# Batch two's first block by fp32 products and TensorE transposes, loads ahead queued behind the bias tiles, the DMA queue in source order later, z shared evenly

## The chip, the cores and the metric

One core of a Trainium2 chip runs the whole program. The metric is the device time of one execution in microseconds, and the median of several runs is quoted. TensorE (PE, with its weight loads as PEld), VectorE (DVE), ScalarE (ACT) and GpSimd (POOL) each run their own instruction stream; SyncE (SP) issues nearly all transfers. Sixteen DMA engines serve the core.

## The reference

The program is attention with a learned bias over relative position, followed by a two-layer network. There are 4 batches, 8 heads, 576 tokens and 64 channels per head.

```
scores = q @ k.T / 8 + bias[head]          # bias = relu(x @ w1 + b1) @ w2, x = log1p|i-j| / log1p(max(i,1))
attn   = exp(scores - max) / (sum + 1e-9)
x      = (attn @ v), heads side by side    # 2304 tokens x 512
h      = x @ w_in                          # 512 -> 2048
out    = (h * clip(h + 3, 0, 6) / 6) @ w_out   # 2048 -> 512
```

All inputs and the output are fp32; the two weight matrices arrive as float64 and are turned into pairs of fp16 parts inside the program.

## The kernel before, in words

**Tiles.** Heads go in four pairs `p`. Attention is cut into units `(b, p, u)`: block `u=0` holds the first 256 tokens of a batch, `u=1` the other 320. All `u=0` units of the four batches come first, then all `u=1` units. A `u=0` unit has four softmax tiles of 128 rows by 576 keys, a `u=1` unit has five, so tiles are numbered n = 0 to 143: batch one's first block is n = 0 to 15, batch two's first block n = 16 to 31, all first blocks end at n = 63.

**A tile on the split path** (all but n = 0 to 15): q and k are split into two fp32r parts (`split_qk_a` on ACT, `split_qk_b` on POOL), the scores are three products (`qk_step`), `soft_max` on DVE adds the bias and finds the row maximum, `soft_exp` on ACT takes the exponent, `soft_norm` and `soft_low` write the normalised tile as two fp16 parts (`hl`: one part by ACT or POOL, the other by DVE, after two small DVE steps), `soft_turn` transposes them by DMA into `at`, and `pv_step` multiplies by v, which is split too (`split_v_a`, `split_v_b`, with two DMA copies). `x_high` and `x_low` write x as two fp16 parts.

**A tile on the direct path** (`direct(b, p, t)`, n = 0 to 15): fp32 products of q and k as loaded (`load_qk0`), the same softmax steps, then five TensorE transposes of the unnormalised tile into PSUM and one ACT copy to SBUF (`soft_low`), and fp32 products with v (`pv_first`). The row sums are inverted for four tiles at once and spread by four small products; `x_first` multiplies.

**Bias.** The bias rows are made in 36 groups of 16 query rows: four `z` tiles (a relu of 128 by 576, by ACT or DVE as the strings `z0`, `z1`, `zeng` say: `z_group`), sixteen TensorE passes (`bias_mm`), an ACT evacuation and a store to DRAM (`bias_out`). Groups 0 to 15 are made before the first tile, beside the preparation of `w_in`. The other 20 are needed only from n = 64 on. They are made by `steps(gen_b, ...)`, 1.1 half steps a tile, two half steps a group, once `phase` is 2; what is missing when the first `u=1` bias tile is to be loaded, at n = 59, is made there at once (`bias_until(S)`). `load_bias` fetches bias tiles up to six tiles ahead.

**The network.** `ffn(b, u)` is a generator: 16 steps of 12 products into `h_ps` and 16 steps of 12 products into `o_ps`, with ACT, DVE and POOL steps (`post`) between them. The block of (0, 0) starts at n = 21 with 4 steps a tile; at its step "w2" the rest of `w_out_prep` is drained. Later blocks go at 2 steps a tile, and 1.55 from n = 64 on. What is not done after the last tile is run at the end.

**Order.** A list scheduler with modelled durations orders each engine's instructions by program order and readiness; it may pull a later instruction forward when the model says that its inputs are there. From n = 21 on TensorE alone keeps program order (`in_order`). At the same point PSUM changes from three double banks for attention and two single banks for the network (`open_psum(stack_p, 3, 2)`) to two and four.

Of the kernel before, what the change touches and what calls it, by code (L numbers as in the profile page):

```python
# [18 lines left out]
S = 576  # L19
# [7 lines left out]
VC = 5 * 128  # L27
CFG = {'z0': 'AD', 'gz': 4, 'z1': 'AAAD', 'gz2': 16, 'zeng': 'AD', 'sg': 'P', 'wm1': 'A', 'wm2': 'A', 'hl': 'AP', 'gl': 'PP', 'vm': 'A', 'g0': 16, 'rwi': 3.0, 'rw0': 1.0, 'rw1': 1.3, 'ro': 3.0, 'rb': 1.1, 'rf0': 4.0, 'rf': 2.0, 'rf1': 1.55, 'la': 6, 'gq': 2, 'gap': -8.0, 'wu': 8, 'act': '', 'tv': 'A', 'pw': 0, 'po': 0, 'gr': 'AD'}
F64_BIAS = 2.0 ** -112
# [4 lines left out]
def attention_moe_kernel(  # L34
# [47 lines left out]

    out_open = [False, 0]
    queue = []
# [12 lines left out]
    eye_sb = const.tile([128, 128], F32, name="eye_sb")  # L97
    r_sb = const.tile([128, 2, PAIRS * 4], F32, name="r_sb")
    wi = big.tile([128, 2, KC, DFF], F16, name="wi")
# [63 lines left out]
    def v_scale(b):  # L163
        parts = const.tile([128, PAIRS], F32, tag="vparts", name="vparts")
        for p in range(PAIRS):
            t = st_p.tile([128, VC], F32, tag="vs", bufs=2, name="va")
            dq("v").dma_start(out=t, in_=vp[b, p])
# [187 lines left out]

    def load_qk0(p):
        t = qk_p.tile([128, 512 + S], F32, tag="hi", name="qk0")
        q, k = t[:, 0:512].rearrange("p (a b) -> p a b", a=2), t[:, 512:512 + S]
        for s in range(2):
            rows = slice(64 * s, 64 * s + 64)  # L360
            dq("q").dma_start(out=q[rows, s], in_=qk[0, p][rows, 0:256])
            nc.gpsimd.memset(q[rows, 1 - s], 0.0)
        dq("q").dma_start(out=k, in_=qk[0, p][:, 256:256 + S])
        qk_t[0, p, 0] = (t, k)

# [41 lines left out]
    def load_v(b, p, u):  # L407
        if (b, u) == (0, 0):
# [3 lines left out]
        dq("v").dma_start(out=t, in_=vp[b, p])  # L412
        v_t[b, p, u] = t
# [24 lines left out]
    def load_bias(b, p, i):  # L438
# [19 lines left out]
        if i < 4:  # L458
            for r in range(2):
                rows = slice(64 * r, 64 * r + 64)  # L460
                if (p, i) not in KEEP:
                    dq("b").dma_start(out=out[rows], in_=bias_d[2 * i + r][:, 2 * p:2 * p + 2, :])
                    continue
                for s in range(2):
                    dq("b").dma_start(out=src[s][rows], in_=bias_d[2 * i + r][:, 2 * p + s, :])
        else:
            for s in range(2):
                dq("b").dma_start(
                    out=out[64 * s:64 * s + 64, 0:S], in_=bias_d[8][:, 2 * p + s, :]
                )  # L470
        return out, src

# [18 lines left out]
    def qk_step(n):  # L491
# [3 lines left out]
        if direct(b, p, t):  # L495
            ps = s_bank("s_ps")
            q, k = qk_t[0, p, 0]
            c = 256 * s + 128 * i
# [41 lines left out]
    def soft_exp(n):  # L540
        bt, sm = a_t[n]
        b, p, t = tiles[n]
        total = r_sb[:, 0, 4 * p + t:4 * p + t + 1] if direct(b, p, t) else sm[:, 1:2]
        nc.scalar.activation(  # L544
# [27 lines left out]
    def direct(b, p, t):  # L572
        return b == 0 and t < 4

# [51 lines left out]

    def pv_first(p):
        at, v = at_t.pop((0, p, 0)), v_t.pop((0, p, 0))
        n = 256
        ps = s_bank("pv_ps")  # L630
        for c in range(5):
            k = slice(64 if c == 4 else 0, 128)
            for s in range(2):
# [5 lines left out]
                )  # L639
        total, r = (r_sb[:, k, 4 * p:4 * p + 4] for k in range(2))  # L640
        nc.vector.tensor_scalar(out=total, in0=total, scalar1=1e-9, scalar2=None, op0=ALU.add)
        nc.vector.reciprocal(out=r, in_=total)
        for t in UT[0]:
# [4 lines left out]
            )  # L648
        pv_t[0, p, 0] = ps

    def x_first(p):
        ps = pv_t.pop((0, p, 0))
        n = 256
        x = x_tile(0, 0)
        xr = hl_p.tile([128, 2, n], F32, tag="hl", name="xr")
        xs, rb = xr[:, 0], xr[:, 1]
        nc.scalar.activation(
            out=rb, in_=ps[:, 1, 0:n], func=AF.Copy, scale=pscale["v0"][1]
        )
# [5 lines left out]
    def pv_step(b, p, u):  # L665
        if direct(b, p, 4 * u):
            return pv_first(p)
        at = at_t.pop((b, p, u))
# [14 lines left out]
    def x_high(b, p, u):  # L683
        if direct(b, p, 4 * u):
            return x_first(p)
        ps = pv_t[b, p, u]
# [203 lines left out]
    def front(n):  # L890
# [3 lines left out]
        if at(n):  # L894
            soft_max(n)
        if n == SWITCH:
            open_steady()
# [140 lines left out]
    phase = 0  # L1038
    SWITCH = 21
    in_order = tc.manual_schedule(engines={mybir.EngineType.PE})  # L1040

    def open_steady():
        nonlocal phase
        drain(gen_w)
        hidden_scale(0)
        for c in range(KC):
            xv = x_t[0, 0][:, :, c]
            nc.vector.tensor_scalar(
                out=xv, in0=xv, scalar1=pscale["r1"][:, c:c + 1], scalar2=None, op0=ALU.mult
            )  # L1050
        stack_a.close()
        del pools["a"], pools["w"]
        stack_p.close()
        open_psum(ctx, 2, 4)
# [4 lines left out]
        in_order.__enter__()  # L1059

    for g in range(cfg["g0"]):
# [3 lines left out]
        if 0 <= g - cfg["gq"] < PAIRS:  # L1065
            load_qk0(g - cfg["gq"])
# [31 lines left out]
    for q_ in queue:  # L1098
        drain(q_)
    in_order.__exit__(None, None, None)  # L1100

# [55 lines left out]
```

## Time and profile before

| what | value |
|---|---|
| median of 3 runs | 739.45 us (733.67 to 739.86) |
| profiled execution, its own time | 735.63 us |
| span of the profiled execution | 733.8 us, so 1.8 us lie around it |
| mean granted TensorE clock | 0.944 |
| PE busy | 639.8 us (87%), 5490 instructions |
| DVE busy | 504.9 us (69%) |
| ACT busy | 509.9 us (69%) |
| POOL busy | 272.3 us (37%) |
| DMA | 133.98 MB, mean 183 GB/s |

A busy PE is not PE at its peak: products overlap in its pipeline, and their ends are modelled. The rate of PE is read from the distance between starts or from a run of many products, not from the mean of one. The page's share of busy time is an average over stages with different limits; the table of stages below, cut at tile numbers, is of more use.

### The profile page before, as it was taken

Reading aid. Unit: us, or ns where it says so; the run is one execution under the profiler, and the core shown is the slowest. Engines: PE = TensorE matmul, PEld = TensorE weight load, DVE = VectorE, ACT = ScalarE, POOL = GpSimd, SP = SyncE. Lnnn points to the kernel's source line nnn. Section 1 sums busy time; section 2 is a strip of 40 time slices with the busy share of each in tenths; the row PEclk is TensorE's granted clock in tenths of the full one; section 3 lists DMA queues with packets and bytes.
Section 4 is the critical chain, followed back from the end, with each engine's and each line's share of the span. In section 5 each row is a group of like instructions: output and inputs, shape, how many; then the busy total and the mean of one; then the engine's idle time right before and its main releaser. Section 6 shows DMA issues by size and latency. Waiting matters only on the chain. (4 is left out here: it accounts for less than half of the span.)

```text
span 733.8 us, 15486 instructions
## 1 busy us (share of the span) xinstructions
PE 639.8 (87%) x5490; PEld 456.6 (62%) x5490; DVE 504.9 (69%) x1274; ACT 509.9 (69%) x1025; POOL 272.3 (37%) x358
## 2 busy tenths in 40 slices
PE   6766487585698999878999898999999999999998
PEld 2213355374365777656777787767776777777775
DVE  6778699999875787457577877787668766730310
ACT  6997487578785898569756885687669866841530
POOL 3111033646031354125443662465246524430420
PEclk9799699689698999989999999999999999999999
DMA  7999686996399999977999999977998785620000
GB/s 221 399 326 338 165 252 177 261 210 159 94 209 258 227 212 196 235 163 180 217 218 220 184 208 192 213 165 161 178 205 166 163 181 118 106 58 19 10 10 28
DMA packets 194062, 133.98 MB, mean 183 GB/s; under 512 B 158144, under 2 KB 166592, under 8 KB 193984
## 3 DMA queue, kind: packets, MB, share of 16 engines
q1 hardware_dynamic: 189376, 128.27, 74.6%
q10 hardware_dynamic: 4608, 4.72, 2.2%
q8 instruction: 43, 0.70, 0.4%
q14 instruction: 35, 0.29, 0.1%
HBM read 75.74 MB, written 15.34 MB: 124 GB/s over the span
## 5 line engine op out<-in xcount | busy, mean ns | idle before, releaser
L747 PE MATMUL h_ps<-x,wi 128*128 128x256 f16 (+1 forms) x1536 | 201.3, 290 | 12.9 <-DVE t L730 5.9
L770 PE MATMUL o_ps<-g,wo 128*128 128x256 f16 (+1 forms) x1536 | 200.4, 290 | 5.5 <-DVE x L137 2.8
L747 PEld LDWEIGHTS <-wi 128*128 128x128 f16 x1536 | 148.4, 99 | 62.3 <-issue 18.5
L770 PEld LDWEIGHTS <-wo 128*128 128x128 f16 x1536 | 149.2, 99 | 53.4 <-issue 11.4
L726 POOL TENSOR_TENSOR g<-t,g 128x256 f16<-128x256 f32 (+1 forms) x128 | 104.4, 824 | 147.3 <-ACT g L724 145.8
L544 ACT ACTIVATE bt<-bt,sm 128x576 f32<-128x576 f32 x144 | 110.5, 768 | 47.2 <-DVE sm L534 46.5
L137 DVE SCALAR_TENSOR_TENSOR hl<-bt,sm,hl 128x576 f16<-128x576 f32 x128 | 113.7, 900 | 32.2 <-POOL hl L114 17.5
L114 POOL TENSOR_SCALAR hl<-bt,sm 128x576 f16<-128x576 f32 x64 | 56.5, 883 | 121.7 <-DVE sm L556 45.8
L730 DVE SCALAR_TENSOR_TENSOR t<-t,t,h_ps 128x320 f32<-128x320 f32 (+1 forms) x112 | 56.5, 516 | 54.5 <-ACT t L737 53.2
L831 PE MATMUL b_ps<-z,w_sb 128*32 128x288 f32 x576 | 68.6, 455 | 22.7 <-ACT z L818 20.3
L724 ACT ACTIVATE g<-t 128x256 f16<-128x256 f32 (+1 forms) x128 | 55.8, 439 | 37.7 <-DVE t L730 36.5
L386 POOL TENSOR_TENSOR qkl<-st,qkh 128x576 fp32r<-128x576 f32 (+2 forms) x56 | 66.1, 1199 | 34.7 <-ACT qkh L379 25.0
L737 ACT ACTIVATE t<-h_ps,t,hr 128x320 f32<-128x320 f32 (+1 forms) x112 | 64.4, 585 | 5.1 <-PE h_ps L747 4.3
L818 ACT ACTIVATE z<-T,bp 128x576 f32<-128x576 f32 x84 | 62.9, 779 | 7.0 <-DVE w2s L203 3.8
L534 DVE CUSTOM_DVE_ANT_0 bt<-s_ps,bt 128x576 f32<-128x576 f32 x80 | 58.3, 750 | 3.0 <-PE s_ps L522 2.8
L831 PEld LDWEIGHTS b_ps<-z,w_sb 128*32 128x32 f32 x576 | 20.6, 114 | 62.9 <-ACT z L818 45.1
L120 ACT ACTIVATE hl<-bt,sm 128x576 f16<-128x576 f32 x64 | 49.3, 770 | 13.5 <-DVE sm L556 6.2
L552 DVE TENSOR_SCALAR sm<-sm 128x1 f32<-128x1 f32 x128 | 18.9, 149 | 55.1 <-ACT bt L544 54.8
L534 DVE CUSTOM_DVE_ANT_0 bt<-s_ps,k 128x576 f32<-128x576 f32 x64 | 46.1, 751 | 9.4 <-DMA k<-bias 6.3
L522 PE MATMUL s_ps<-qkh 64*128 64x288 f32 x224 | 34.2, 356 | 15.0 <-DVE sm L534 6.7
L780 ACT ACTIVATE ot<-o_ps,os 128x256 f32<-128x256 f32 (+1 forms) x32 | 15.8, 493 | 41.4 <-PE o_ps L770 40.7
L243 POOL TENSOR_SCALAR w<-w 128x512 f32<-128x512 f32 x22 | 16.0, 731 | 66.8 <-ACT cu L241 59.3
(115 smaller groups left out, 852.7 us busy)
## 6 DMA issues: line engine op xcount, KB each, us to landing
bt<-bias SPq DMA_DIRECT2D x64, 288.0 KB, 4.9
bias<-bo SPq DMA_DIRECT2D x36, 288.0 KB, 5.5
vs<-in_vp_dram SPq DMA_DIRECT2D x28, 320.0 KB, 4.0
w<-in_w_in_dram SPq DMA_DIRECT2D x16, 512.0 KB, 7.4
st<-in_qk_dram SPq DMA_DIRECT2D x16, 448.0 KB, 4.9
va<-in_vp_dram SPq DMA_DIRECT2D x16, 320.0 KB, 6.1
wo<-in_w_out_dram SPq DMA_DIRECT2D x10, 512.0 KB, 6.1
st<-in_qk_dram SPq DMA_DIRECT2D x12, 416.0 KB, 5.2
```

Source lines behind the costliest of these rows:

```text
L114: nc.gpsimd.tensor_scalar(out=out, in0=full, scalar1=scale, scalar2=1.0, op0=ALU.mult, op1=ALU.mult)
L137: nc.vector.scalar_tensor_tensor(out=out, in0=full, scalar=scale, in1=high, op0=ALU.mult, op1=ALU.subtract)
L386: nc.gpsimd.tensor_sub(out=lo[:, c:c + w], in0=t[:, c:c + w], in1=hi[:, c:c + w].bitcast(F32))
L534: nc.vector.tensor_tensor_reduce(out=halves(bt), in0=ps, in1=halves(src), op0=ALU.add, op1=ALU.min, scale=-0.125, scalar=3.0e38, accum_out ...
L544: nc.scalar.activation(out=bt, in_=bt, func=AF.Exp, scale=-1.0, bias=sm[:, 0:1], accum_out=total)
L726: e.tensor_sub(out=g[:, 1], in0=uu, in1=g[:, 0])
L730: nc.vector.scalar_tensor_tensor(out=t_t[f], in0=t_t[f], scalar=cols(f)[2], in1=h_t.pop(f)[:, 0:n], op0=ALU.min, op1=ALU.mult,)
L737: nc.scalar.activation(out=t_t[f], in_=h_t[f][:, 0:n], func=AF.Relu, scale=cols(f)[0], bias=cols(f)[1],)
L747: nc.tensor.matmul(out=h_t[f][:, 0:n], lhsT=wi[:, a, c, f * 128:(f + 1) * 128], rhs=x[:, e, c], start=(k == 0), stop=(k == 3 * KC - 1),)
L770: nc.tensor.matmul(out=ops[:, 0:n], lhsT=wo[:, a, f, e * 128:(e + 1) * 128], rhs=g_t[f][:, r], start=(f == 0 and a == 0 and r == 0), stop= ...
L818: nc.scalar.activation(out=z, in_=src, func=AF.Relu, bias=bp[:, col])
L831: nc.tensor.matmul(out=pss[a][32 * k:32 * k + 32, 0:HALF], lhsT=w2_sb, rhs=z[:, a * HALF:(a + 1) * HALF],)
```

## The change: what it does

`fb` becomes 2: units (1, p, 0) take the direct path too, n = 0 to 31. The FFN of (0, 0) still opens at n = 21 (`START`), now with 2 steps a tile and with no pause after "w2"; `phase` stays 1 there, so bias groups 16 to 35 wait. PSUM keeps its first layout, and TensorE the scheduler's order, until `SWITCH` = 37, where the open block is drained, `phase` becomes 2, PSUM is laid out anew and TensorE keeps program order. The `z` tiles before the first tile alternate between ACT and DVE (`z1` was three to one); later ones go DVE, DVE, ACT. Loads of q, k, v are ordered on SP behind the latest bias tile load that the program has traced, loads of `w_out` behind the fourth. From n = 44 on SP keeps program order.

```diff
-CFG = {'z0': 'AD', 'gz': 4, 'z1': 'AAAD', 'gz2': 16, 'zeng': 'AD', ... 'rf0': 4.0, ... 'gap': -8.0, ...}
+CFG = {'z0': 'AD', 'gz': 12, 'z1': 'AD', 'gz2': 16, 'zeng': 'DDA', ... 'rf0': 2.0, ... 'gap': 0.0, ... 'wb': 3, 'fb': 2, 'spn': 44}
...
-        elif out_open[0]:
+        elif out_open[0] and steady[0]:
...
+    bias_loads = []
+
+    def behind(k=-1):
+
+        return tc.issue_after(bias_loads[k]) if len(bias_loads) > max(k, 0) else nullcontext()
...
-        dq("w").dma_start(out=t, in_=src.bitcast(U32))
+        with behind(cfg["wb"]) if k is not None else nullcontext():
+            dq("w").dma_start(out=t, in_=src.bitcast(U32))
...
-        dq("k").dma_start(out=t, in_=qk[b, p][:, 256 * u:256 * u + w])
+        with behind():
+            dq("k").dma_start(out=t, in_=qk[b, p][:, 256 * u:256 * u + w])
...
     def direct(b, p, t):
-        return b == 0 and t < 4
+        return b < cfg["fb"] and t < 4
...
+        if n == START:
+            open_ffn()
         if n == SWITCH:
             open_steady()
...
-        if l == 0 and k + 2 < len(units) and k + 2 >= PAIRS:
-            load_qk(*units[k + 2])
-        if k + 1 < len(units) and k + 1 >= PAIRS:
+        if l == 0 and PAIRS <= k + 2 < len(units):
+            b2, p2, u2 = units[k + 2]
+            if direct(b2, p2, 4 * u2):
+                load_direct(b2, p2)
+            else:
+                load_qk(b2, p2, u2)
+        if k + 1 < len(units) and not direct(units[k + 1][0], 0, 4 * units[k + 1][2]):
...
-    SWITCH = 21
-    in_order = tc.manual_schedule(engines={mybir.EngineType.PE})
+    START, SWITCH = 21, 16 * cfg["fb"] + 5
+    in_order = ctx.enter_context(ExitStack())
+
+    def keep_order(*names):
+        engines = {getattr(mybir.EngineType, e) for e in names}
+        in_order.enter_context(tc.manual_schedule(engines=engines))
...
+    def open_steady():
+        nonlocal phase
+        if SWITCH > START:
+            while queue:
+                r = next(queue[0], "end")
+                if r == "w2":
+                    drain(gen_o)
+                if r == "end":
+                    queue.pop(0)
+            phase = 2
+        stack_p.close()
+        open_psum(ctx, 2, 4)
+        steady[0] = True
+        keep_order("PE")
...
+        if n == cfg["spn"]:
+            keep_order("SP")
...
-                    phase = 2
+                    phase = 2 if steady[0] else 1
```

`pv_first`, `x_first` and `load_qk0` (now `load_direct`) take the batch as an argument, and a vector `x1` carries batch two's scale for v times that for `w_in`.

## Rows read from the trace of the kernel before

**Rows 1.** Stages: from:to length, then busy us and count by engine, PEclk, DMA, GB/s

```profile
0.00:64.70 64.70, 45.96 (x284) 15.03 (x284) 49.48 (x112) 55.91 (x84) 12.46 (x26) 0.89 0.95 327
64.70:81.40 16.70, 3.50 (x15) 1.94 (x14) 9.32 (x20) 6.22 (x12) 2.18 (x3) 0.74 0.99 256
81.40:120.10 38.70, 31.32 (x190) 22.05 (x190) 38.06 (x120) 32.05 (x64) 12.61 (x14) 0.94 0.68 191
120.10:190.00 69.90, 43.92 (x349) 32.65 (x351) 66.26 (x178) 47.96 (x97) 35.78 (x42) 0.80 0.81 201
190.00:227.30 37.30, 34.08 (x354) 24.23 (x354) 25.05 (x73) 28.39 (x53) 8.20 (x10) 0.93 0.81 180
227.30:369.00 141.70, 128.11 (x1268) 95.50 (x1263) 95.85 (x230) 108.91 (x226) 54.59 (x72) 0.93 0.91 208
369.00:485.20 116.20, 108.63 (x1040) 88.51 (x1039) 88.42 (x223) 84.74 (x187) 53.60 (x73) 1.00 0.97 198
485.20:733.80 248.60, 244.30 (x2006) 176.71 (x2002) 132.47 (x326) 145.73 (x306) 92.87 (x122) 1.00 0.54 113
```

**Rows 2.** The line of `soft_max`, stretch 0 to 227.2: counts, first and last start

```profile
L534 DVE CUSTOM_DVE_ANT_0 bt<-s_ps,bt x27: 726/751/759, 64.7 to 226.6; 128x576 f32<-128x576 f32 x27
L534 DVE CUSTOM_DVE_ANT_0 bt<-s_ps,k x10: 743/751/758, 81.4 to 216.7; 128x576 f32<-128x576 f32 x10
```

**Rows 3.** Chain that ended last, late part: start, length, what, how many

```profile
492.08 0.98 PE s_ps L522 x12
...
704.27 26.09 PE o_ps L770 x192
```

**Rows 4.** Timeline of DVE: the third tile's `soft_max` and its wait

```profile
81.43 0.76 DVE L534 CUSTOM_DVE_ANT_0 bt<-s_ps,k 128x576 f32<-128x576 f32 x1 [6.29 <-DMA k<-bias]
```

**Rows 5.** Timeline of SP's queue: loads ahead, and the bias tile waited for

```profile
23.13 2.64 SPq L373 DMA_DIRECT2D st<-in_qk_dram  x2
...
49.28 2.01 SPq L229 DMA_DIRECT2D wo<-in_w_out_dram  x2
...
73.41 1.09 SPq L465 DMA_DIRECT2D k<-bias  x2
```

**Rows 6.** Lines by form, whole span: busy us, mean ns, idle before

```profile
L137 DVE SCALAR_TENSOR_TENSOR hl<-bt,sm,hl 128x576 f16<-128x576 f32 x128 | 113.7, 900 | 32.2 <-POOL hl L114 17.5 <-ACT hl L120 13.8 <-DMA at<-hl 0.3
...
L818 ACT ACTIVATE z<-T,bp 128x576 f32<-128x576 f32 x84 | 62.9, 779 | 7.0 <-DVE w2s L203 3.8 <-DVE bp L986 3.0 <-PE b_ps L831 0.2
...
L552 DVE TENSOR_SCALAR sm<-sm 128x1 f32<-128x1 f32 x128 | 18.9, 149 | 55.1 <-ACT bt L544 54.8
```

**Rows 7.** The line of `z` on DVE before the first tile: ns min/median/max

```profile
L814 DVE TENSOR_SCALAR z<-T,nbp x20: 505/516/917, 5.3 to 59.7; 128x576 f32<-128x576 f32 x20
```

**Rows 8.** Timeline of PE at full clock: products of the direct path

```profile
103.14 1.24 PE L500 MATMUL s_ps<-qk 128*128 128x288 f32 x4
104.22 0.71 PE L592 MATMUL t_ps<-eye_sb,bt 128*128 128x128 f32 x5
...
109.05 2.53 PE L634 MATMUL pv_ps<-atf,vf 128*64 128x256 f32 x20
111.51 0.66 PE L645 MATMUL pv_ps<-eye_sb,r_sb 128*64 128x128 f32 x8
112.09 1.24 PE L500 MATMUL s_ps<-qk 128*128 128x288 f32 x4
```

**Rows 9.** Timeline of PE: v products of a split unit, then FFN products

```profile
166.69 1.17 PE L675 MATMUL pv_ps<-at,vh 128*64 128x256 f16 x18
...
168.34 2.79 PE L747 MATMUL h_ps<-x,wi 128*128 128x256 f16 x24
```

**Rows 10.** Timeline of PE at n = 59: two bias groups in a row

```profile
345.90 1.18 PE L831 MATMUL b_ps<-z,w_sb 128*32 128x288 f32 x16
349.04 3.27 PE L831 MATMUL b_ps<-z,w_sb 128*32 128x288 f32 x16 [1.97 <-ACT z L818]
```

**Rows 11.** Timeline of ACT near n = 52: a wait for a load

```profile
306.46 0.52 ACT L399 ACTIVATE tq<-st 64x64 fp32r<-64x64 f32 x2 [8.30 <-DMA st<-in_qk_dram]
```

More of the change, by code (lines that the diff above doesn't have):

```diff
@@ L1 @@
-from contextlib import ExitStack, contextmanager
+from contextlib import ExitStack, contextmanager, nullcontext
 from itertools import chain
@@ L83, in attention_moe_kernel @@
     out_open = [False, 0]
+    steady = [False]
     queue = []
@@ L97, in attention_moe_kernel @@
     eye_sb = const.tile([128, 128], F32, name="eye_sb")
-    r_sb = const.tile([128, 2, PAIRS * 4], F32, name="r_sb")
+    r_sb = const.tile([128, 2, 2 * PAIRS * 4], F32, name="r_sb")
     wi = big.tile([128, 2, KC, DFF], F16, name="wi")
@@ L166, in v_scale @@
             t = st_p.tile([128, VC], F32, tag="vs", bufs=2, name="va")
-            dq("v").dma_start(out=t, in_=vp[b, p])
+            with behind():
+                dq("v").dma_start(out=t, in_=vp[b, p])
             yield
@@ L360, in load_qk0 @@
             rows = slice(64 * s, 64 * s + 64)
-            dq("q").dma_start(out=q[rows, s], in_=qk[0, p][rows, 0:256])
+            with behind():
+                dq("q").dma_start(out=q[rows, s], in_=qk[b, p][rows, 0:256])
             nc.gpsimd.memset(q[rows, 1 - s], 0.0)
-        dq("q").dma_start(out=k, in_=qk[0, p][:, 256:256 + S])
-        qk_t[0, p, 0] = (t, k)
+        with behind():
+            dq("q").dma_start(out=k, in_=qk[b, p][:, 256:256 + S])
+        qk_t[b, p, 0] = (t, k)
     QW = (256, 320)
@@ L372, in load_qk @@
         t = st_p.tile([128, 1024], F32, tag="st", name="st")[:, 0:w]
-        dq("k").dma_start(out=t, in_=qk[b, p][:, 256 * u:256 * u + w])
+        with behind():
+            dq("k").dma_start(out=t, in_=qk[b, p][:, 256 * u:256 * u + w])
         st_t[b, p, u] = t
@@ L407, in load_v @@
     def load_v(b, p, u):
-        if (b, u) == (0, 0):
+        if direct(b, p, 4 * u):
             t = v_p.tile([128, VC], F32, tag="vh", name="vf")
@@ L411, in load_v @@
             t = st_p.tile([128, VC], F32, tag="vs", bufs=2, name="vs")
-        dq("v").dma_start(out=t, in_=vp[b, p])
+        with behind():
+            dq("v").dma_start(out=t, in_=vp[b, p])
         v_t[b, p, u] = t
@@ L461, in load_bias @@
                 if (p, i) not in KEEP:
-                    dq("b").dma_start(out=out[rows], in_=bias_d[2 * i + r][:, 2 * p:2 * p + 2, :])
+                    d = dq("b").dma_start(
+                        out=out[rows], in_=bias_d[2 * i + r][:, 2 * p:2 * p + 2, :]
+                    )
                     continue
                 for s in range(2):
-                    dq("b").dma_start(out=src[s][rows], in_=bias_d[2 * i + r][:, 2 * p + s, :])
+                    d = dq("b").dma_start(
+                        out=src[s][rows], in_=bias_d[2 * i + r][:, 2 * p + s, :]
+                    )
         else:
             for s in range(2):
-                dq("b").dma_start(
+                d = dq("b").dma_start(
                     out=out[64 * s:64 * s + 64, 0:S], in_=bias_d[8][:, 2 * p + s, :]
                 )
+        bias_loads.append(d.ins)
         return out, src
@@ L542, in soft_exp @@
         b, p, t = tiles[n]
-        total = r_sb[:, 0, 4 * p + t:4 * p + t + 1] if direct(b, p, t) else sm[:, 1:2]
+        k = 16 * b + 4 * p + t
+        total = r_sb[:, 0, k:k + 1] if direct(b, p, t) else sm[:, 1:2]
         nc.scalar.activation(
@@ L625, in attention_moe_kernel, with pv_first @@
     pv_t = {}
-    def pv_first(p):
-        at, v = at_t.pop((0, p, 0)), v_t.pop((0, p, 0))
+    def pv_first(b, p):
+        at, v = at_t.pop((b, p, 0)), v_t.pop((b, p, 0))
         n = 256
@@ L639, in pv_first @@
                 )
-        total, r = (r_sb[:, k, 4 * p:4 * p + 4] for k in range(2))
+        total, r = (r_sb[:, k, 16 * b + 4 * p:16 * b + 4 * p + 4] for k in range(2))
         nc.vector.tensor_scalar(out=total, in0=total, scalar1=1e-9, scalar2=None, op0=ALU.add)
@@ L648, in pv_first, with x_first @@
             )
-        pv_t[0, p, 0] = ps
-    def x_first(p):
-        ps = pv_t.pop((0, p, 0))
+        pv_t[b, p, 0] = ps
+    def x_first(b, p):
+        ps = pv_t.pop((b, p, 0))
         n = 256
-        x = x_tile(0, 0)
+        x = x_tile(b, 0)
         xr = hl_p.tile([128, 2, n], F32, tag="hl", name="xr")
@@ L657, in x_first @@
         nc.scalar.activation(
-            out=rb, in_=ps[:, 1, 0:n], func=AF.Copy, scale=pscale["v0"][1]
+            out=rb, in_=ps[:, 1, 0:n], func=AF.Copy,
+            scale=pscale["x1"][:, p:p + 1] if b else pscale["v0"][1],
         )
@@ L666, in pv_step @@
         if direct(b, p, 4 * u):
-            return pv_first(p)
+            return pv_first(b, p)
         at = at_t.pop((b, p, u))
@@ L684, in x_high @@
         if direct(b, p, 4 * u):
-            return x_first(p)
+            return x_first(b, p)
         ps = pv_t[b, p, u]
@@ L1050, in open_steady @@
             )
+        if cfg["fb"] > 1:
+            x1 = const.tile([128, KC], F32, name="x1")
+            nc.vector.tensor_scalar(
+                out=x1, in0=pscale["r1"], scalar1=pscale["v1"][1], scalar2=None, op0=ALU.mult
+            )
+            pscale["x1"] = x1
         stack_a.close()
         del pools["a"], pools["w"]
-        stack_p.close()
-        open_psum(ctx, 2, 4)
         pools["g"] = ctx.enter_context(tc.tile_pool(name="g", bufs=1, reuse_waits="tile"))
```

13 lines of the change are left out of this document (6 added, 7 removed).

## The prediction

> **What bounds the kernel now.** I read the stage table first, cut at tile numbers: the line of `soft_max` has 27 + 10 = 37 records before 227.2, so n = 37 starts there [rows 2]; n = 0, 2 and 16 start at 64.7, 81.4 and 120.1, n = 64 at 369.0 and n = 99 at 485.2. Four regimes are to be seen in [rows 1]. Up to 81.4 the DMA engines are full (0.95 and 0.99), and ACT is busy 55.9 of 64.7. From 81.4 to 190 DVE is busy 38.1 of 38.7 and 66.3 of 69.9: it carries the softmax tiles and the float64 weights. From 227 to 369 PE is busy 128 of 141.7, with stalls and a clock of 0.93. From 369 on PE is busy 108.6 of 116.2 and 244.3 of 248.6: what is left is a queue of products, and time saved earlier reaches the end only if PE stands earlier at the same product.
>
> So I price the change by when n = 37 and n = 64 begin; after that PE's order is the same as before.
>
> **Before n = 16.** n = 2 waits for a bias tile: DVE's last 6.29 us of idling end on it [rows 4], and PE is busy 3.5 us in the whole 16.7 [rows 1]. The tile's first transfers were issued at 73.41, in a queue into which loads for later had gone: q and k of batch two at 23.13, `w_out` at 49.28 [rows 5]. The change puts such loads behind bias loads on SP. Nothing is gained if the bias store is late for other reasons; at most n = 2 follows n = 0 as closely as later tiles do, 2.8 us a tile (38.7 for 14), which saves 11. I take 9. The `z` share takes 12 tiles from ACT at 0.779 (9.3) [rows 6] and gives DVE 12 at 0.516 (6.2) [rows 7]. In this stretch DVE idles 64.7 - 49.5 = 15.2, so it has room; ACT's gain is bounded by 0 and 9.3, and as DMA was full too I take 2. n = 16 then starts at 109 (range 103 to 118).
>
> **From n = 16 to 37: DVE.** A direct tile does without the low part (0.900) and two small steps (0.149 shown, its twin taken as equal) [rows 6]: 16 x 1.2 = 19.2. Four low parts of v go, 4 x 0.9 = 3.6, the price of the nearest row, which is 576 wide instead of 640. Two small steps a unit come back, 1.2. x is one DVE pass either way. Bias groups wait for n = 37: 11 tiles x 1.1 half steps are six groups, 12 `z` on DVE, another 6.2, which cancels the `z` gained earlier. DVE's busy time up to n = 37 was 188.2 [rows 1]; it becomes 188.2 - 21.6 = 166.6. Idle was 227.3 - 188.2 = 39.1: 15.2 before n = 0, 7.4 in the stall, 4.2 between 81 and 190, 12.3 after. The stall's goes, and DVE, lighter, will wait a little more elsewhere: I keep 38, so DVE allows n = 37 at about 205.
>
> **The same stretch: PE.** A direct tile costs 1.08 (103.14 to 104.22) + 0.71 + a quarter of 2.46 + 0.58, together 2.55 [rows 8]; a split one half of 0.98 [rows 3] and a quarter of 1.65 (166.69 to 168.34) [rows 9], 0.90. So PE gets 16 x 1.65 = 26.4 us more work. From n = 16 to 37 it has 16 x 2.55 + 5 x 0.90 = 45.3, and the first network block, 384 products at 2.79 / 24 = 0.116 [rows 9], 44.6: 90 us, which from 109 gives 199 with no gap and 209 at 90% busy. Before, PE had 21 x 0.90 + 44.6 + six bias groups at 1.18 [rows 10], 70.6, in 107.2. The cover is that idle time; without it the 26.4 would be paid in full. DVE and PE meet at 205 (190 to 222); I take 205.
>
> The first block's products now have two single PSUM banks instead of four. A bank is free after one ACT and one DVE pass, at most 0.779 + 0.516 by wider tiles [rows 6, 7]: eight pairs, 0 to 10 us. Direct tiles fill the gaps, so I take 0. The Trainium skill (Perfetto Trace Analysis, Optimizing Tensor Performance, Matmuls) says that independent groups should rotate through different banks so that evacuation overlaps the next group; two banks still rotate, but by that rule I would lean to the 10, and the sum would be 10 higher.
>
> **Small items.** ACT gets 16 PSUM copies (0.779 each at most [rows 6]), loses half of the `hl` parts, four copies each of q/k and v, and its share of six bias groups; it was busy 170.5 of 227.3 [rows 1], so: nothing. POOL loses eight subtractions and gains eight memsets at 71 busy of 227: nothing. SP loses 16 transposes and eight v copies and gains eight loads, issued before they are due: nothing; uncovered, a late q/k load would cost a transfer's some 8 us once, as the row of a late load shows [rows 11]. With TensorE's order free until n = 37, products can pass one that waits; I count that in the 38.
>
> **From n = 37 to 64** (141.7 before). Six more bias groups cost PE 7.1 if it is full, nothing if they fall into its 13.6 idle: 5. Walking the loop's counters, groups 16 to 27 are made by n = 58 and the last eight at once at n = 59, where it was two. PE keeps program order there, and the second of two adjacent groups starts 3.14 after the first, for 1.18 of work [rows 10]: 1.96 idle, six more times, 11.8. Against this, ACT stood 8.30 for a load that the scheduler had thought early [rows 11]; SP in source order from n = 44 should end such misjudged pulls forward: 8 (0 to 14). 141.7 + 5 + 11.8 - 8 is 150 (138 to 165); n = 64 starts at 355.
>
> **From n = 64 on** (364.8 before). 36 network steps are left after the last tile instead of 39, by the same counters: 3 x 12 x 26.09 / 192 = 4.9 less [rows 3]. Of PE's 11.9 idle in the last two stages I give SP's order 3 (0 to 8; it could also lose, where a transpose waits behind a bias store: 4). 364.8 - 4.9 - 3 is 357.
>
> **Sum.** 205 + 150 + 357 = 712 span, 22 below 733.8. With 1.8 around it, 714 against the profiled 735.6; the median of the runs lies 3.8 above that execution, so I predict 718.
>
> **Rivals.**
> *PE pays for its new work.* If the 90 us run at the 0.73 that PE was busy from 120.1 to 227.3 (78.0 of 107.2 [rows 1]), n = 37 comes at 232: 745 less what a fuller stretch leaves idle later, some 5, so 740, no change. For it: two PSUM banks and clocks of 0.80 and 0.93 there. Against: DVE, which held PE up there, loses 21.6.
> *The order edges do little.* If transfers stay as late and ACT's pulls forward stay, 9 + 8 are lost: 735, no change. For it: a bias tile also waits for its store, which the change does not move.
> *The burst at n = 59, slower than before.* Four `z` of a group and their products share two double buffers, and ACT and DVE also serve the softmax. If a group takes 7 us instead of 3.14, eight idle 8 x 5.8 - 3.9 = 43, 31 more than summed: 749. It decides from 6.8 a group on. For it: the pair shown had already one wait of 1.97 inside the second group, with one predecessor [rows 10]. Against: `z` now leans on DVE, which is busy 96 of 141.7.
> *The clock.* From 81.4 to 120.1 the granted clock was 0.94, nearly the full 2.4 GHz, with direct tiles all along [rows 1]; at 1.2 GHz a direct tile would take 5.1, 16 of them 41 more: 758. The Trainium skill (TensorE: Matmul & The Clock Gate, Part 4: PE-mode transpose) says that the full clock does not engage for transposes; by that rule this rival would come, and the trace disagrees as long as other products stand between them, here 0.94.
> *More than summed.* The burst hides in softmax work and DVE idles only 25: 205 - 13 and 150 - 12 give 693.
>
> **How the numbers follow.** Forecast 0.53 (its own range 703 to 731); more 0.10; PE pays 0.13; edges do little 0.10; burst 0.11; clock 0.03. About 1% (7.4 us) is what a measurement of this kernel can tell from no change: faster, below 732, 0.63; within, 0.23; slower, above 747, 0.14. The range 698 to 744 leaves out the two slow rivals, and half of the fast one.
>
> **What would show it.** n = 2 at 70 or earlier, with no wait of DVE for a bias tile; n = 16 near 109; DVE's busy time up to n = 37 near 167, and n = 37 near 205; 16 x 5 transposes at a granted clock near 1; eight bias groups in a row on PE with gaps of 2 to 3 us near n = 59; no wait of ACT for q/k loads over 3 us after n = 44; PE without a gap after n = 99. It is wrong if n = 37 comes after 220, or if the stretch to n = 64 takes over 165.

## The result and the profile after

The changed kernel takes 741.87 us, the median of 18 runs, and the kernel before 735.67 beside it: a ratio of 1.0086, with a 95% interval from 1.006 to 1.0111. The prediction said 718 and faster; it is slower by 0.9%. The profiled execution has a span of 739.6 us (733.8 before) and a mean granted clock of 0.96 (0.944 before).

The stages of the kernel after, cut at the starts of tiles n = 0, 2, 16, 37, 40, 60, 64 and 99; columns as in [rows 1]:

```profile
0.00:59.10 59.10, 39.64 (x280) 13.51 (x280) 49.77 (x117) 45.98 (x68) 12.31 (x26) 0.88 0.89 279
59.10:68.10 9.00, 4.44 (x13) 2.97 (x14) 8.04 (x21) 6.81 (x13) 2.47 (x4) 0.81 0.71 241
68.10:110.10 42.00, 33.62 (x184) 23.40 (x185) 34.25 (x102) 26.91 (x55) 6.63 (x13) 0.88 0.96 280
110.10:188.70 78.60, 71.19 (x511) 51.30 (x511) 72.44 (x205) 63.13 (x131) 31.83 (x39) 0.96 0.70 196
188.70:232.10 43.40, 38.59 (x327) 30.96 (x324) 21.16 (x62) 21.56 (x43) 10.20 (x14) 0.88 0.62 144
232.10:329.30 97.20, 88.46 (x931) 67.32 (x933) 69.45 (x171) 74.68 (x155) 38.70 (x51) 0.96 0.78 169
329.30:370.60 41.30, 34.33 (x314) 20.08 (x304) 19.73 (x47) 26.57 (x51) 9.68 (x14) 0.96 0.56 143
370.60:492.30 121.70, 110.28 (x1026) 88.67 (x1022) 89.02 (x224) 86.27 (x190) 52.67 (x74) 0.99 1.01 213
492.30:739.60 247.30, 241.36 (x1978) 174.25 (x1974) 132.39 (x324) 143.32 (x302) 89.96 (x120) 1.00 0.54 115
```

The same view of the kernel before, from n = 37 to 64, now cut at n = 40 and n = 60 as well:

```profile
227.30:248.70 21.40, 18.10 (x153) 12.47 (x148) 14.81 (x37) 15.19 (x29) 3.84 (x6) 0.84 1.06 266
248.70:346.50 97.80, 89.48 (x928) 67.94 (x930) 67.38 (x163) 78.08 (x165) 37.79 (x50) 0.95 0.85 192
346.50:369.00 22.50, 20.53 (x197) 15.08 (x190) 13.66 (x34) 15.64 (x34) 12.96 (x17) 0.92 1.02 218
```

Read the starts of the stages first. The changed kernel is ahead by 10.0 us at n = 16 (110.1 against 120.1), by 38.6 at n = 37, by 16.6 at n = 40 and by 17.2 at n = 60. At n = 64 it is behind by 1.6, and at the end by 5.8. So nearly everything that the change earned lies in front of n = 40, and it is lost between n = 60 and 64, where 22.5 us became 41.3; a further 4.2 go from there to the end.

These starts are DVE's. PE is the busiest engine from n = 60 on, so read it too, at the scores of the same tiles. Here are the scores of n = 64 and n = 99, in the kernel before and then in the kernel after:

```profile
365.79 0.53 PE L522 MATMUL s_ps<-qkh 64*128 64x288 f32 x4
...
482.75 0.40 PE L522 MATMUL s_ps<-qkh 64*128 64x288 f32 x1
```

```profile
365.94 0.53 PE L540 MATMUL s_ps<-qkh 64*128 64x288 f32 x4
...
490.83 0.54 PE L540 MATMUL s_ps<-qkh 64*128 64x288 f32 x4
```

PE is ahead by 17.25 us at the scores of n = 60 (327.66 against 344.91), level at those of n = 64, and behind by 8.1 at those of n = 99. So PE loses 17.4 us between n = 60 and 64 and 8 more up to n = 99.

**The large lead at n = 37 is not real.** It shrinks to 16.6 in three tiles, because the second half of the first network block runs there. PE of the kernel before, around that half (start, length, instruction, and in brackets the idle time before it and what ended it):

```profile
188.34 0.37 PE L148 MATMUL m_ps<-eye_sb,m_w 128*1 128x128 f32 x1 [10.66 <-DVE m_w L143]
...
200.42 1.48 PE L770 MATMUL o_ps<-g,wo 128*128 128x256 f16 x12
...
240.60 2.79 PE L770 MATMUL o_ps<-g,wo 128*128 128x256 f16 x24
```

And PE of the kernel after:

```profile
190.14 0.27 PE L149 MATMUL m_ps<-eye_sb,m_w 128*1 128x128 f32 x1
...
199.99 1.44 PE L790 MATMUL o_ps<-g,wo 128*128 128x256 f16 x6 [1.94 <-ACT g L121]
202.52 22.01 PE L790 MATMUL o_ps<-g,wo 128*128 128x256 f16 x186 [1.10 <-DVE g L119]
...
230.91 0.53 PE L540 MATMUL s_ps<-qkh 64*128 64x288 f32 x4
```

The 192 `o_ps` products begin at 200.42 before and 199.99 after: the change did not move them. They need `w_out`, whose preparation ends in a maximum that passes from DVE over PE and back twice. Before, PE stood 10.66 us for the first step of that (`m_w`). After, DVE has `m_w` at 185.31, and PE, now full of direct tiles, takes it up only at 190.14. The chain of small steps took 2.8 us before (188.14 to 190.95) and takes 12.6 after. Some 6.3 of them are waits for PE's two steps, the second of which starts at 192.34; 5.2 more follow it on DVE, which does softmax and v steps between the small ones. Here are the chain's two ends on DVE of the kernel after:

```profile
185.31 0.14 DVE L144 TENSOR_REDUCE m_w<-w2p 128x1 f32<-128x16 f32 x1
...
197.92 0.22 DVE L212 TENSOR_SCALAR r_w2c<-w2p,rm_w 128x16 f32<-128x16 f32 x1
```

Tiles up to n = 39 ran ahead meanwhile and then waited for the block. What remains as gain is that the block ends at 224.5 instead of 243.4.

**The loss at n = 59.** PE of the kernel after, where the late bias groups are made in a row:

```profile
328.65 1.18 PE L851 MATMUL b_ps<-z,w_sb 128*32 128x288 f32 x16
331.82 4.16 PE L851 MATMUL b_ps<-z,w_sb 128*32 128x288 f32 x20 [1.99 <-ACT z L838]
336.43 1.17 PE L851 MATMUL b_ps<-z,w_sb 128*32 128x288 f32 x12 [0.46 <-ACT z L838]
...
349.81 1.16 PE L851 MATMUL b_ps<-z,w_sb 128*32 128x288 f32 x10 [0.45 <-ACT z L838]
350.90 2.79 PE L767 MATMUL h_ps<-x,wi 128*128 128x256 f16 x24
```

Eight groups take 22.25 us (328.65 to 350.90), 2.8 each, less than the 3.14 from one to the next in [rows 10]. SP's queue over the same time (start, time from first to last issue, what, how many):

```profile
327.39 25.45 SPq L869 DMA_DIRECT2D bias<-bo  x9
352.93 1.12 SPq L475 DMA_DIRECT2D bt<-bias  x2
354.10 0.58 SPq L385 DMA_DIRECT2D st<-in_qk_dram  x1
354.72 0.43 SPq L425 DMA_DIRECT2D vs<-in_vp_dram  x1
355.19 6.48 SPq L628 DMA_TRANSPOSE at<-hl  x2
361.72 2.51 SPq L480 DMA_DIRECT2D k<-bias  x4
```

For 25.45 us SP issues nine bias stores and nothing else, as it keeps the order of the program from n = 44 on. Each store waits for ACT's evacuation of its group, and the next unit's bias tile, q/k and v, and the kept bias tiles, wait behind them; from 240 to 370 SP stood 51.6 us for such evacuations. This is that wait (us in total, times, longest), and behind it the same one in the second experiment below, where source order is taken away:

```profile
SPq L869 <- ACT bo L867: 51.6, 15, 8.8
```

```profile
SPq L869 <- ACT bo L867: 13.3, 9, 3.3
```

The late v loads come back as waits. ACT from n = 64 to 99, waits by releaser (columns as in the last rows):

```profile
ACT bt L563 <- DVE sm L552: 19.4, 15, 3.5
ACT vh L121 <- DMA vs<-in_vp_dram: 10.9, 5, 3.1
```

In the kernel before no wait of ACT for v is listed in that stretch.

### The profile page after: what moved, and what is told of

Same layout as the page of the kernel before. It is cut to its first block, busy times and chain, and to the rows that moved or that the text cites. A ratio compares the mean times of both kernels' runs of the same rounds, so it can differ in the third digit from the quotient of the medians.

```text
span 739.6 us, 15489 instructions
## 1 busy us (share of the span) xinstructions
PE 661.9 (89%) x5538; PEld 472.5 (64%) x5538; DVE 496.3 (67%) x1263; ACT 495.2 (67%) x1004; POOL 254.4 (34%) x350
## 5 line engine op out<-in xcount | busy, mean ns | idle before, releaser
L767 PE MATMUL h_ps<-x,wi 128*128 128x256 f16 (+1 forms) x1536 | 203.9, 290 | 17.2 <-DVE x L138 8.2
L790 PE MATMUL o_ps<-g,wo 128*128 128x256 f16 (+1 forms) x1536 | 197.5, 288 | 5.7 <-ACT g L121 1.9
L767 PEld LDWEIGHTS <-wi 128*128 128x128 f16 x1536 | 148.9, 99 | 66.7 <-issue 17.8
L746 POOL TENSOR_TENSOR g<-t,g 128x256 f16<-128x256 f32 (+1 forms) x128 | 100.9, 797 | 159.2 <-ACT g L744 157.4
L138 DVE SCALAR_TENSOR_TENSOR hl<-bt,sm,hl 128x576 f16<-128x576 f32 x112 | 98.7, 894 | 30.7 <-POOL hl L115 18.4
L115 POOL TENSOR_SCALAR hl<-bt,sm 128x576 f16<-128x576 f32 x56 | 46.4, 829 | 132.6 <-DVE sm L575 37.5
L851 PE MATMUL b_ps<-z,w_sb 128*32 128x288 f32 x576 | 64.2, 462 | 22.5 <-ACT z L838 19.3
L398 POOL TENSOR_TENSOR qkl<-st,qkh 128x576 fp32r<-128x576 f32 (+2 forms) x48 | 55.7, 1180 | 25.9 <-ACT qkh L391 23.0
L518 PE MATMUL s_ps<-qk 128*128 128x288 f32 x128 | 41.1, 447 | 13.7 <-DVE sm L552 7.5
L834 DVE TENSOR_SCALAR z<-T,nbp 128x576 f32<-128x576 f32 x85 | 45.7, 578 | 9.2 <-PE b_ps L851 7.0
L121 ACT ACTIVATE hl<-bt,sm 128x576 f16<-128x576 f32 x56 | 43.1, 769 | 6.0 <-ACT t L757 2.1
L838 ACT ACTIVATE z<-T,bp 128x576 f32<-128x576 f32 x59 | 44.7, 767 | 3.1 <-DVE bp L1012 2.9
L571 DVE TENSOR_SCALAR sm<-sm 128x1 f32<-128x1 f32 x112 | 16.7, 150 | 44.8 <-ACT bt L563 44.7
```

The source lines that it names most:

```text
L115: nc.gpsimd.tensor_scalar(out=out, in0=full, scalar1=scale, scalar2=1.0, op0=ALU.mult, op1=ALU.mult)
L138: nc.vector.scalar_tensor_tensor(out=out, in0=full, scalar=scale, in1=high, op0=ALU.mult, op1=ALU.subtract)
L398: nc.gpsimd.tensor_sub(out=lo[:, c:c + w], in0=t[:, c:c + w], in1=hi[:, c:c + w].bitcast(F32))
L746: e.tensor_sub(out=g[:, 1], in0=uu, in1=g[:, 0])
L767: nc.tensor.matmul(out=h_t[f][:, 0:n], lhsT=wi[:, a, c, f * 128:(f + 1) * 128], rhs=x[:, e, c], start=(k == 0), stop=(k == 3 * KC - 1),)
L790: nc.tensor.matmul(out=ops[:, 0:n], lhsT=wo[:, a, f, e * 128:(e + 1) * 128], rhs=g_t[f][:, r], start=(f == 0 and a == 0 and r == 0), stop= ...
```

## The experiments

Ratios are to the kernel before, run beside them, with 95% intervals. Starts of tiles are those of `soft_max` in the profiled execution; stage lengths are thus from one execution of each kernel, while the ratios are from 6 to 18.

**The suspects at n = 59, one at a time.** First the eight groups: bias groups made faster per tile, so that none is left at n = 59.

```diff
-'rb': 1.1
+'rb': 1.9
```

> The changed kernel with 1.9 half steps of bias a tile instead of 1.1 from n = 37 on, so that the 20 late groups are made one by one before n = 59 and none is left for the moment when the first u=1 bias tile is loaded. Theory (the eight groups in a row at n = 59 are what the change pays with: their two tiles took 34.0 us against 15.1 before): n = 60 to 62 falls from 34.7 to under 17, tiles from 40 to 58 get some 5 us longer, the time falls by 10 to 16 us, to 726 to 732, ratio to before 0.985 to 0.995. Rival (PE is full from n = 40 on and the groups cost the same wherever they stand): the two tiles get shorter, the others longer by as much, and the time stays at 739 to 743, ratio 1.005 to 1.01.

Measured: 0.9915 (0.9883 to 0.9946), span 724.1. Without the row of eight the loss is gone and 1.7% more comes.

Then source order taken away:

```diff
-'spn': 44
+'spn': 999
```

> The changed kernel without source order on SP (the scheduler orders SP's queue to the end). Theory (source order delays transfers from n = 64 on; the stretch from n = 64 to the end took 369.0 us against 364.8 before, although three network steps fewer were left): that stretch falls to 360 to 364 and the time by 4 to 8 us, ratio to before 0.998 to 1.004. Rival (source order saves waits for loads that were pulled forward, as the prediction had it): the time rises by 3 to 8 us, ratio 1.012 to 1.02, and waits of ACT for q/k loads over 5 us come back between n = 44 and 64.

Measured: 0.9885 (0.9839 to 0.9931), span 727.0. n = 60 to 64 takes 36.3 us instead of 41.3, n = 40 to 60 takes 93.2 instead of 97.2, and the rest 365.0 instead of 369.0. SP in source order, which the prediction booked as a gain of 8 + 3, costs 2%. That is more than this theory had: of 13.0 us from n = 40 on, 4.0 lie before n = 60, 5.0 up to n = 64 and 4.0 behind it.

Both together:

```diff
-'rb': 1.1, ... 'spn': 44
+'rb': 1.9, ... 'spn': 999
```

> The changed kernel with 1.9 half steps of bias a tile and without source order on SP. Measured singly against the changed kernel's ratio of 1.0086 to before, the first gave 0.9915 and the second 0.9885, 1.7 and 2.0% less. Theory (source order costs mostly in the burst, where SP stood for one bias store after the other from 327 to 352 us while loads waited; without the burst there is little for it to hold up): together 2.2 to 2.8% less than the changed kernel, 721 to 726, ratio 0.980 to 0.987. Rival (two costs that have nothing to do with each other): together 3.7% less, 713 to 717, ratio 0.970 to 0.974.

Measured: 0.9871 (0.9838 to 0.9904), span 725.2. The two edits do not add: either takes back nearly all. So the loss is for the most part their meeting. In this kernel the groups move into n = 40 to 60, which takes 113.3 instead of 93.2, and n = 60 to 64 takes 14.8 instead of 36.3: without source order, and with the order edges in place, eight groups in a row cost no more than the same groups spread out. Without the edges they do, as the run on `z` below shows.

**Where source order costs.** Source order only after the groups at n = 59 have been issued, and, as another kernel, source order from n = 44 but the last eight stores issued by ACT:

```diff
-'spn': 44
+'spn': 60
```

> The changed kernel with SP in source order only from n = 60 on, after the eight bias groups at n = 59. Theory (source order costs in the burst alone): 0.985 to 0.992, span 725 to 730, kept bias tiles loaded from about 300 on. Rival (it also costs from n = 64 on, 3.5 us of the 12.6 between the two spans): 0.993 to 1.0, span 730 to 734.

```diff
-        dq("o").dma_start(
+        (nc.scalar if g >= 28 else nc.sync).dma_start(
```

> The changed kernel with one edit: the stores of the last eight bias groups are issued by ACT, which makes what they store, and no longer by SP; SP's source order and the eight groups in a row stay. Theory (the loss is SP standing for these stores, with loads queued behind them): about what source order taken away gave, 0.985 to 0.993, q, k, v and kept bias tiles issued during the burst. Rival (source order costs in itself, by holding transposes and loads in the order of the program also after the burst): 1.002 to 1.011, as the changed kernel.

Measured: order from n = 60 on gives 0.9888 (0.9855 to 0.992), span 726.6, the same as no order at all. It is neither a gain nor a loss after the burst. SP's queue of this kernel (columns as above) shows loads of kept bias tiles among the stores:

```profile
323.68 0.54 SPq L869 DMA_DIRECT2D bias<-bo  x1
326.37 1.09 SPq L480 DMA_DIRECT2D k<-bias  x2
327.84 9.20 SPq L869 DMA_DIRECT2D bias<-bo  x4
338.92 0.45 SPq L480 DMA_DIRECT2D k<-bias  x1
```

With the eight stores on ACT: 0.9974 (0.9946 to 1.0003), span 735.2, between theory and rival. SP's queue of this kernel goes on with the loads at once:

```profile
330.38 0.33 SPq L869 DMA_DIRECT2D bias<-bo  x1
330.80 1.11 SPq L475 DMA_DIRECT2D bt<-bias  x2
331.96 0.58 SPq L385 DMA_DIRECT2D st<-in_qk_dram  x1
332.58 0.42 SPq L425 DMA_DIRECT2D vs<-in_vp_dram  x1
```

and its ACT from n = 64 to 99 waits 1.0 us for v instead of 10.9:

```profile
ACT vh L121 <- DMA vs<-in_vp_dram: 1.0, 2, 0.6
```

From n = 64 on it takes 365.1, so this part of the loss was the stores. But SP still stood 31.3 us for the stores of earlier groups, and n = 48 to 52 still takes 20.7 us, as after the change (16.7 with SP free). So all twenty late stores were moved (`g >= 16` in the line above):

> The changed kernel with the stores of all twenty late bias groups issued by ACT, not only of the last eight; SP's source order from n = 44 on stays. With eight moved SP still stood 31.3 us for the other stores, of 51.6, and half of the loss came back. Theory (SP standing for stores is the whole loss of source order): 0.985 to 0.992, span 725 to 730, n = 60 near 325. Rival (the other half is source order itself, transposes and loads held in the order of the program): 0.995 to 1.0, n = 60 at 329 or later.

Measured: 0.9935 (0.9904 to 0.9965), span 728.7. n = 48 to 52 takes 16.6 now. From n = 40 to the end the changed kernel takes 507.5 us, with eight stores moved 501.2, with twenty 499.7, without source order before n = 60 494.6. Of the 12.9 that source order costs there, 7.8 went with the stores that SP no longer issues; 5.1 are left. The ratios say the same less sharply: 1.5 of the 2.0% came back, and the intervals of 0.9935 and 0.9888 overlap. The span and the start of n = 60 (325.6) are the theory's, the ratio lies between it and the rival again. In this run SP stood 13.8 us for bias stores to land ahead of kept bias tiles (one wait of 11.2), with the next instructions behind it; that these waits are the 5.1 is not shown, nor whether ACT loses by issuing the stores.

**The direct path.** Undone alone, with all else of the change kept:

```diff
-'rf0': 2.0, ... 'gap': 0.0, ... 'fb': 2
+'rf0': 4.0, ... 'gap': -8.0, ... 'fb': 1
```

> The changed kernel with batch two's first block on the split path again, the network's first block at 4 steps a tile and the pause after w2, so PSUM and TensorE's order switch at n = 21 and bias groups start again at n = 26; z share, the order edges and source order on SP stay. Theory (the direct path of batch two wins some 16 us by n = 40 and loses more by the groups it puts off): the eight groups in a row are gone, n = 16 stays near 110, n = 40 comes near 240, the time is 727 to 733, ratio to before 0.988 to 0.996. Rival (the late groups are not what costs; SP's order and the edges are): the time stays at 739 to 745.

Measured: 1.0146 (1.0103 to 1.019), span 746.8. Theory and rival both fell. There is no burst of eight groups here, yet it is the slowest but one, and most of that is lost before n = 40, which comes at 258.7 instead of 248.7: PE, in program order from n = 21 on, stood 17.8 us for the maximum over `w_out` (10.66 before), which DVE had at 196.2 instead of 188.1. The last load of `w_out` ahead of it was issued at 188.3 instead of 177.3; that the order edges are the reason is likely and not shown. Then the direct path alone, with no order edges (`behind` returns `nullcontext()`), SP free, and z shared as before:

```diff
-'gz': 12, 'z1': 'AD', ... 'zeng': 'DDA', ... 'spn': 44
+'gz': 4, 'z1': 'AAAD', ... 'zeng': 'AD', ... 'spn': 999
```

> The direct path for batch two's first block alone, with what it brings along (bias groups delayed to tile 37, eight of them at once at tile 59): no order edges, SP free, z shared as before. Theory (the direct path is the gain, edges and source order are losses, z is worth nothing): 0.976 to 0.983, span 716 to 721, n = 40 near 229. Rival (the gain before n = 40 needs the edges or the new z share as well): 0.988 to 1.0, n = 40 later than 234.

Measured: 0.9911 (0.988 to 0.9943), span 730.2, n = 40 at 230.6. The ratio is the rival's, but not for its reason: n = 40 is where the theory put it, 18.1 ahead of the kernel before, so the whole lead comes from the direct path and what it brings along. It is lost in n = 60 to 64 (39.6 us), though SP is free here. Source order costs without the edges too: 0.9911 here against 1.0036 in the changed kernel without them (below), `z` aside.

**z shared evenly.** No edges, SP free, groups at 1.9, with the old share (`'gz': 4, 'z1': 'AAAD', 'zeng': 'AD'`):

> Bias groups at 1.9 half steps a tile, SP free, no order edges (0.9757), and z shared as before the change. Theory (the new share is worth nothing, ACT and DVE have room where z is made): 0.973 to 0.979, span 713 to 717. Rival (it takes ACT off the path before the first tile, or DVE's new load costs later): outside of that, by 3 us or more, with n = 0 or n = 64 moved by as much.

Measured: 0.9776 (0.9741 to 0.9811), against 0.9757 with the new share. n = 0 starts at 61.2 instead of 48.9, n = 64 at 350.4 instead of 348.7. Twelve microseconds at the first tile are worth about two later, and in the time nothing that can be told.

This kernel differs from the direct path alone (0.9911) by nothing but 1.9 half steps for 1.1. So with SP free and no edges the row of eight groups does cost something: 1.3% of the time, and n = 40 to 64 takes 133.0 with it and 122.1 without.

**The order edges.** All of them taken away from the changed kernel, and from the one with spread groups and SP free:

```diff
-        return tc.issue_after(bias_loads[k]) if len(bias_loads) > max(k, 0) else nullcontext()
+        return nullcontext()
```

> The changed kernel without the order edges: loads ahead and loads of w_out are not queued behind bias loads. Theory (the first product of the network's second half began at 200.4 before and at 200.0 after, set by the end of the w_out preparation on DVE, so an earlier n = 16 is not worth its size): n = 2 comes near 80 again and n = 16 some 8 us later, but n = 40 moves by under 4, ratio to before 1.004 to 1.014. Rival (the edges' gain reaches the end): the time rises by 8 to 10 us, ratio 1.018 to 1.023.

> The kernel of both edits, and without the order edges as well. Theory (with the edges the w_out loads come some 15 us later and the w_out preparation ends at 188 instead of 183, which sets when the network's second half starts; alone this was worth 0.5%): another 0.3 to 0.7% less than with both edits. Rival (the edges' earlier n = 2, 68 instead of 77, reaches the end once the burst is gone): 0.5 to 1.2% more.

Measured: 1.0036 (1.0005 to 1.0067) from 1.0086, and 0.9757 (0.9711 to 0.9802) from 0.9871. The edges do for n = 2 what was forecast: with them it starts at 66.5 instead of 76.4. At n = 16 only 3.0 of that are left (108.4 against 111.4; 2.6 in the changed kernel, 110.1 against 112.7), at n = 40 nothing (230.8 with, 229.3 without), and in the end the edges cost 0.5 to 1.1%. They cost nothing beside the row of eight with SP free: 0.9885 with both, 0.9911 with the row alone (and the old share of `z`), 0.9871 with the edges alone, 0.9757 with neither. Either is enough to lose over 1%; why they do not add is open. Which edge, from the same kernel with spread groups and SP free; first without the one on `w_out`, then with that one alone:

```diff
-        with behind(cfg["wb"]) if k is not None else nullcontext():
+        with nullcontext():
```

> Bias groups at 1.9 half steps a tile and SP free, with the order edges on the loads of q, k and v kept and the edge on the loads of w_out dropped. Theory (the edges cost by holding q and k loads late: ACT stood 6.7 us for one near tile 55 with all edges): 0.984 to 0.990, as with all edges (0.9871). Rival (the edge on w_out costs, as its preparation sets when the network's second half starts): 0.974 to 0.979, as without any (0.9757).

```diff
-    def behind(k=-1):
+    def behind(k=-1, on=False):
...
-        with behind(cfg["wb"]) if k is not None else nullcontext():
+        with behind(cfg["wb"], True) if k is not None else nullcontext():
```

(`behind` gives an edge only where `on` is set.)

> Bias groups at 1.9 half steps a tile, SP free, and of the order edges only the one on the loads of w_out. Theory (this edge alone costs, as the run without it gave 0.9757 and with it 0.9871): 0.983 to 0.990. Rival (it costs only together with the edges on q, k and v, or the step between the two runs came from the order that the scheduler happened to pick): 0.973 to 0.980.

Measured: edges on q, k and v alone 0.9757 (0.9727 to 0.9787); the edge on `w_out` alone 0.9793 (0.9759 to 0.9828). The theory of the first, that late q and k loads cost, fell: ACT's waits for them were 11.4 us with all edges and 9.3 here, and the time is that without any edge. The theory of the second fell too. Only both kinds together cost 1.1%; the intervals of the others overlap. How they combine is not settled.

**Bias groups early.** From n = 26 on, while the first network block waits for its weights, with SP free (`'spn': 999`), in PSUM of the scores as long as the first layout stands:

```diff
-        if phase:
+        if steady[0]:
...
-        bias_ps[g] = pss if phase else ps
+        bias_ps[g] = pss if steady[0] else ps
...
+            if n >= 26:
+                steps(gen_b, ab, cfg["rb"])
```

> The changed kernel without source order on SP, with 1.1 half steps a tile, but with the bias groups made from n = 26 on, as before, also while the network's first block is open (in a double bank of attention's PSUM then). Theory (what matters is that no eight groups are left for n = 59; before n = 37 DVE is full, so six groups there cost it 12 to 16 z of 0.5 us): the network's second half starts 4 to 8 us later than 200, n = 60 to 62 takes under 18, ratio 0.980 to 0.990, within 0.5% of the kernel of both edits. Rival (bias groups before n = 37 are free): 1% or more under the kernel of both edits.

> The bias groups early and SP free, as in the run that gave 0.9799, and now without any order edge on loads. Theory (edges delay loads of q, k and v that are then due, and cost about 1.1% once burst and source order are gone): 0.967 to 0.974, span about 710. Rival (with the bias groups out of the way before the 40th tile the loads have slack, so the edges cost nothing): 0.977 to 0.983, span 716 to 719.

Measured: 0.9799 (0.9759 to 0.984) with the edges and 0.9757 (0.9728 to 0.9785) without, each between its theory and its rival. The network's second half did not start later, as the first theory had it, but at 186.2 instead of 200.0. With the edges the groups are better early than spread from n = 37 on (0.9871), by 0.7% with intervals that just touch; without them there is no difference (0.9757 both).

**One that told nothing.** The kernel before with SP in source order from n = 44 on:

```diff
+    in_sp = tc.manual_schedule(engines={mybir.EngineType.SP})
...
+        if n == 44:
+            in_sp.__enter__()
```

> The kernel before with source order on SP from n = 44 on, and nothing else of the change. Theory (source order costs where bias stores wait in the queue; before there is a burst of two groups, and stores at every other tile up to n = 59): 3 to 8 us more, ratio 1.004 to 1.011, and stretches after n = 64 cost nothing. Rival (source order costs its 14 us wherever it stands): ratio 1.017 to 1.022. The prediction's view (it saves 8 to 11): ratio 0.985 to 0.99.

Measured: 1.0553 (1.0511 to 1.0595). The scheduler's order changed from the start on: the first load of `w_out` was issued at 144 instead of 49, and PE stood 39.5 us for its maximum. From n = 64 on it takes 366.9 against 364.8. It is no test of source order.

## Why the prediction was wrong, point by point

The sum was 712 of span; 739.6 came. By its own sign it was wrong: the stretch from n = 37 to 64 took 181.9 us, where 165 was the limit. The 3.8 that made 718 of 714 was chance in a median of three: over 18 runs the kernel before has 735.67, its profiled execution 735.63.

- **Before n = 16: right in sum, by luck in its parts.** n = 16 at 109 was predicted, 110.1 came; n = 2 starts at 68.1, without the wait for a bias tile that [rows 4] shows. But the 9 booked for the order edges are 2.6 to 3.0 at n = 16 in the runs without them, and the 2 booked for the `z` share are 5.2 (111.4 against 116.6, both without edges).
- **DVE up to n = 37: right in work, wrong in what it means.** 166.6 us busy were predicted, 164.5 came. n = 37 was to start at 205 and started at 188.7, but the step "PE, the same stretch" counted the first block's 384 products in front of n = 37, and half of them come behind it: they wait for `w_out`, and PE reached its maximum late. The lead that counts is 16.6 at n = 40, not 22.3: 5.7 of the miss.
- **PE pays for its new work.** The rival at 740 has the time but not the place: PE is busy 71.2 of 78.6 from n = 16 to 37, where it allowed the tiles to run ahead. What the fuller engines cost is the 12.6 us chain of `w_out`, about half of it on PE and the rest on DVE. That two PSUM banks cost up to 10 us is not borne out by these rows.
- **The clock.** Granted 0.96 from 110.1 to 188.7, with 91 of the 160 TensorE transposes there, and 1.00, the full 2.4 GHz, up to 178.0: the rival is refuted. The Trainium skill (TensorE: Matmul & The Clock Gate, Part 4: PE-mode transpose) says that the full clock does not engage for them; with fp32 and fp16 products between them it did.
- **The eight groups: right in size and mechanism, for PE.** 3.14 us a group were assumed, 2.8 came; the rival's 7 did not. With SP free from n = 44 to 60, the stretch from n = 40 to 64 is 8.9 longer than before (129.2 against 120.3), where the sum had 16.8 without SP's gain: 7.9 in favour. Read on PE, with source order taken away, the scores of n = 60 to those of n = 64 take 37.7 us instead of 20.9, which is the 16.8; the gain came before, between n = 40 and 60, and was in no term. What the sum did not ask is whether the groups could be spread: without edges that is worth 1.3%.
- **SP in source order: the step that failed.** The prediction gave it a gain of 8 up to n = 64 and 3 behind. It read one wait of ACT for a load [rows 11] as a load pulled forward too early, and priced source order by that. The longest such wait behind n = 44 did get shorter, from 8.3 us to 2.6, but it is 5.0 without source order, and waits for v, of 4.8 and less, took its place. The runs give no gain and a loss of 12.9 (n = 40 to the end, 507.5 against 494.6). Of the miss of 27.6 this step is 23.9. It bounded the loss by 4, for a transpose behind a bias store behind n = 64, and did not ask what stands behind the very stores that the next item of its sum puts in a row.
- **Fewer steps at the end: two, not three.** Behind the scores of the last tile PE has 600 products of the network left, where it had 624: two steps, 3.3 us by [rows 3]. What follows the last tile is 87.6 us instead of 90.6: 3.0 of the 4.9. But tiles 64 to 143 take 3.6 us longer than before even where source order costs nothing (277.8 against 274.2), so from n = 64 on nothing is gained (365.4 against 364.8): 5.5 of the miss. Of these 3.6, 2.2 are DVE's marker: between the scores of the same tiles PE takes 275.9 instead of 274.5. Where the other 1.4 come from is open.

The rival of the burst (749) has part of the place, but put its price on PE, at 7 us a group. The price lay on SP's queue, which it did not look at: of the 13.0 us that its order costs, 4.0 came due before n = 60, where single groups already held up loads, 5.0 up to n = 64, and 4.0 behind it, where ACT waited for v.

The parts add up to 5.7 + 23.9 - 7.9 + 5.5 = 27.2 of the 27.6; the rest is rounding. Without source order and edges and with the groups spread, the kernel takes 718.84 us, 0.9757 of the kernel before. That this is near the predicted 718 bears out nothing, as spreading was in no term of the sum. Two others share that ratio; none is faster. So the direct path is a gain (0.9911 alone, 0.9757 with the groups spread as well), and source order, the order edges and the row of eight groups cover that gain.

## What to carry to other kernels

When a queue is put into program order, list what in it waits for a computation that is late, and price everything that stands behind that, not only the waits that the new order removes. Two edits can cost next to nothing one by one and lose together: here, with the order edges in place, a row of stores (0.1% without source order) and an ordered queue (0.4% without the row, with intervals that overlap). And such a finding holds for the kernel it was made in: without the edges the row costs 1.3% by itself. And a lead is to be read at a point that all streams of work have passed; a marker of one stream can run ahead of another that it must wait for.

## What the runs showed of the hardware that was not expected

A transfer that waits for an engine holds all that stand behind it on its issuing engine: SP issued nine stores in 25.45 us and no load between them, though the 16 transfer engines were then busy at a share of only 0.24 (327.4 to 352.9).

A lead at the first tile is worth little here: n = 0 started between 47.7 and 61.2 us in the kernels with the direct path for both blocks, and n = 40 between 228.3 and 237.0, in no order with it.
